# Retention and gated feed-forward on one core: another order of reading and writing in the output evacuation, one score moved by a tile, some preparation steps in another order

## The chip, the cores and the metric

The kernel runs on one core of a Trainium2 chip. The metric is the time of one execution on the device in microseconds (us), as the median of several runs. Besides, one execution was recorded by the hardware profiler; all durations of single instructions come from that one. PE is the matrix engine (PEld its weight loads), DVE the vector engine, ACT the scalar engine, POOL the general engine, SP the engine that here issues most of the DMAs.

## The reference, cut to what matters

```python
# q, k, v: [8, 8, 576, 64] f32      (batch, heads, positions, head size)
scores = q @ k.T / sqrt(64)
Dmat[i, j] = gamma_h ** (i - j) if i >= j else 0
x = (scores * Dmat) @ v             # -> [4608 tokens, 512]
h = x @ w_in                        # w_in  [512, 2048]
out = (h * cos(h)) @ w_out          # w_out [2048, 512], out [4608, 512] f32
```

## The kernel before, in words

**Retention.** Tokens are taken in 18 groups G of 256. A group has four chunks of 64 positions. The decay is taken into q and k beforehand (`prep_q`, `prep_k`, line 179, on POOL), so that a chunk needs the masked scores of its own keys (`scores`, line 286, masks at 298 or 302 on DVE), a running state k^T v (`states`, matmuls 359, additions on DVE at 380 and 382, bf16 copies `sb` on ACT at 390 and 391), and output matmuls (`retention`, line 469): "cross" and "same" of queries with the state, "own" of masked scores with values. Between "cross" and the rest stands a nop on ACT (481) that PE waits for. `done` (line 494) evacuates the outputs from PSUM as bf16 into xT, two copies of 128x512 per group: both on ACT, or one on ACT and one on DVE where it is called with `both`. From G=6 (`FINE`) on, queries lie in an order in which four neighbouring tokens are 16 places apart (r, i), and xT takes them in token order (i, r), so the copy has to permute.

k and q are turned by DMA transposes (`turn_k`, `turn_q`, line 205) into kT and qT. `values` (816) casts v to bf16 on ACT. `turned(G)` turns k of G; `quad(Q)` scales the queries of four blocks on POOL; `load`, `load_q` fetch k and v of a group, q of two groups.

**Feed-forward.** Tokens go through in ten tiles n, of 512, 256, 256 and then seven of 512 tokens (n = 3 is `S7`, n = 9 `last`). A tile n >= 3 has two parts. First `mm1` (545): 8 blocks i, each with a PSUM bank of "abm" in turn, cosine on ACT (553), product on DVE (554) into gT. Then `mm2_seven`: the second matmul as seven products of half size (697) in the order 3, 4, 5, 2, 1, 7, 6. Five of them take sums of quarters of gT (`g_sum`, line 624, gs5, gs2, gs1, gs7, gs6), on DVE where the condition `on_dve` holds, otherwise on POOL, with a fence so that a POOL sum comes after the DVE sum before it. The results are put together by ACT copies (742, 747, 752) and DVE additions (722) and stored by SP (729).

**Order of the work.** All of it is written out by hand; each engine runs its instructions in the order of the program. Into tile n >= 3 retention is woven for the next tile's tokens: groups G = 2n and G + 1, and scores for the group after. The table `at` says ahead of which product each step stands. `unit(G)` is retention(G) with the scores and states of G + 1. `begin`/`end` is retention alone; `end(both)` evacuates first on ACT, then on DVE. In tiles 3 and 4 the steps stand at products 5, 1 and 6; in tiles 5 to 7 at 4 and 1. Tile 4 has `unit` also at 6, so that it computes three scores: of 8, 9 and 10.

Preparation is called from three places: `prep_inside(n, i)` after block i of mm1, `sums_after(n, i)` after that for the g_sums, and `feed(s)` after each of the four stores r = 0 (c12), 1 (c21), 2 (u11), 3 (u22) of a tile. In `feed` n counts from 0 for tile 3, so that G = 8 + 2n is the first group of the tile after. Buffers: one gT, one gs of each kind, three of kT, of the bf16 values and of the loaded k and v each, four of scaled k.

Of the kernel before, what the change touches and what calls it, by code (L numbers as in the profile page):

```python
# [17 lines left out]
def kernel(  # L18
# [26 lines left out]
    NP = NG // 2  # L45
# [14 lines left out]
    S7 = 3  # L60
# [349 lines left out]
    def retention(G, bank="m", evac=nc.scalar.copy):  # L410

        if len(bank) == 1:
            ps = psum.tile([P, 2, 2, DG, HP], F32, tag=bank, name="ov")
            outs = [ps[:, x] for x in range(2)]
        else:
            outs = [psum.tile([P, 2, DG, HP], F32, tag=b, name="ov") for b in bank]
        vb = tiles["v", G]
        own, cross, same = [], [], []  # L420
        every = slice(0, 2)
        for y in range(2):
            ret = tiles.pop(("ret", G, y))
            yq = every if G < FINE else slice(y, y + 1)
            for h0 in range(0, H, 2):
                for x in range(2):
                    for h in (h0, h0 + 1):
                        own.append(
                            (
                                h, x, yq, HP, vb[half(x), h, y, :],  # L430
                                ret[half(x), h // HG, blocks_of(G, y, h % HG), :],
                            )
                        )
        before = (steps(G - 1) + steps(G))[-len(steps(G)) - 1 : -1] if G else [None] + steps(0)[:-1]
        for prev, (name, cells, fresh, _) in zip(before, steps(G)):
            _, x, y = name
            mix = (G, x) == (2, 0)
            if prev is None or (fresh and not mix):
                continue
            sb = tiles.pop(("sb", prev[0]))  # L440
            n = QP if mix else HP
            yq = every if y is None else slice(y, y + 1)
            for he in range(2):
                for hg in range(HG):
                    (same if he == x else cross).append(
                        (
                            he * HG + hg, x, yq, n, sb[half(he), hg, :],
                            queries(G, he, hg, x, yq, n),
                        )
                    )  # L450

        def spread(part):

            part.sort(key=lambda u: (u[2].start, u[0] % HG // 2 * 2))
            return part

        parts = {"cross": spread(cross), "own": own, "same": spread(same)}
        begun, left, turn = set(), {}, []
        for part in parts.values():
            for h, x, *_ in part:  # L460
                left[x, h % 2] = left.get((x, h % 2), 0) + 1

        def run(name, switch=False):
            i = None
            for h, x, yq, n, lhsT, rhs in parts.pop(name):
                at = (x, h % 2)
                left[at] -= 1
                dst = outs[x][half(h % 2), yq, h // 2, :n]
                i = nc.tensor.matmul(  # L469
                    dst if name == "own" else as_queries(G, dst),  # L470
                    lhsT=lhsT,
                    rhs=rhs,
                    start=at not in begun,
                    stop=left[at] == 0,
                    skip_group_check=True,
                )
                begun.add(at)
                if turn:
                    fence(i, turn.pop(), "other rows")
            if switch and i is not None:  # L480
                turn.append(nc.scalar.nop())
                fence(turn[0], i, "other rows")

        def done(*evacs):
            xT = x_of(2 * G * P, 2 * P)
            if G < FINE:
                xT = xT.rearrange("p c (x i y) -> p x y c i", x=2, y=2)
            else:
                xT = xT.rearrange("p c (y x i r) -> p x y c r i", x=2, y=2, r=4)
            for x in range(2):  # L490
                ps = outs[x]
                if G >= FINE:
                    ps = ps.rearrange("p y c (r i) -> p y c r i", r=4)
                (evacs or (evac, evac))[x](xT[:, x], ps)  # L494

        return run, done
# [109 lines left out]
    def g_sum(n, x, e0, e1):  # L606

        gT = tiles["g", n]
        a, b, op_ = {
            5: ((0, 0), (0, 1), ALU.add),  # L610
            2: ((1, 0), (1, 1), ALU.add),
            1: ((0, 0), (1, 1), ALU.add),
            7: ((0, 1), (1, 1), ALU.subtract),
            6: ((1, 0), (0, 0), ALU.subtract),
        }[x]
        if ("gs", n, x) not in tiles:
            tiles["gs", n, x] = sump.tile([P, E2, 256], BF16, tag=f"gs{x}", name=f"gs{x}")
        i0, i1 = (
            gT[:, k * E2 + e0 : k * E2 + e1, r * 256 : (r + 1) * 256] for r, k in (a, b)
        )  # L620
        on_dve = x == 5 or (n, x) == (S7, 2) or (n, x, e0) in (
            (S7, 1, 4), (S7 + 1, 2, 4), (last, 1, 0), (last, 2, 4)
        ) or (x == 6 and e0 == 0 and S7 < n < last)
        i = (nc.vector if on_dve else nc.gpsimd).tensor_tensor(  # L624
            out=tiles["gs", n, x][:, e0:e1], in0=i0, in1=i1, op=op_
        )
        if on_dve:
            tiles["gate"] = i
        elif "gate" in tiles:
            fence(i, tiles.pop("gate"), "port free")  # L630

    def sums_after(n, i):

        if n == S7:
            if i < 4:
                w_sums(3 + i % 2, i // 2 * 4, i // 2 * 4 + 4)
            elif i < 6:
                g_sum(n, 5, i % 4 * 4, i % 4 * 4 + 4)
                if i == 5:
                    g_sum(n, 6, 0, 4)  # L640
            elif i == 7:
                g_sum(n, 2, 0, E2)
                g_sum(n, 1, 4, E2)
                g_sum(n, 1, 0, 4)
                for e in (0, 4):
                    g_sum(n, 7, e, e + 4)
                g_sum(n, 6, 4, E2)
        elif n == S7 + 1 and i in (3, 7):
            for x in (5, 2):
                g_sum(n, x, i - 3, i + 1)  # L650
            if i == 7:
                g_sum(n, 6, 0, 4)
            g_sum(n, 1, i - 3, i + 1)
            if i == 7:
                for e in (0, 4):
                    g_sum(n, 7, e, e + 4)
                g_sum(n, 6, 4, E2)
        elif i == 3:
            for x in (5, 2, 1, 7) if n < last else (5, 1, 2, 7, 6):
                g_sum(n, x, 0, 4)  # L660
        elif i == 7 and n == last:
            late_sums(n)
# [155 lines left out]
    def feed(s):  # L818

        n, r = divmod(s - starts[S7] // P, 4)  # L820
        G = 8 + 2 * n
        if n == 0:
            if r == 0:
                load_q(5)
                load(10)
            elif r == 2:
                quad(4)
                turned_q(4)
                prep_k(8, 0)
                prep_k(8, 1)  # L830
                turned(8)
                values(8)
            elif r == 3:
                prep_k(9, 0)
                prep_k(9, 1)
                turned(9)
                values(9)
            return
        if G >= NP:
            return  # L840
        if r == 0:
            values(G)
            if G + 3 < NP:
                load(G + 3)
        if r < 2:
            prep_k(G + 1, r)
        if r == 1 and G + 2 < NP:
            quad(G // 2 + 1)
        if r == 2:
            turned(G + 1)  # L850
        if r == 3:
            values(G + 1)
            if G + 2 < NP:
                turned_q(G // 2 + 1)

    def prep_inside(n, i):
        G = 2 * n + 2
        if n == S7 + 1 and i == 3:
            quad(5)
        if n > S7 and i in (3, 7) and G < NP:  # L860
            prep_k(G, i // 4)
            if i == 7:
                if n == S7 + 1:
                    turned_q(5)
                turned(G)
                if n == S7 + 1:
                    load(11)
                if G + 2 < NP:
                    load_q(G // 2 + 1)
                    load(G + 2)  # L870

    plan = {
# [179 lines left out]
    for n, w in enumerate(widths):  # L1052
# [64 lines left out]
            ]  # L1117
        else:
            at = {}
            if n in (3, 4):  # L1120
                at = {
                    5: lambda acts, flush, later: (flush(), at_once(*ready(G))),
                    1: lambda acts, flush, later: unit(G, acts, flush),
                    6: lambda acts, flush, later: (flush(), begin(G + 1), end(both)),
                }
                if n == 4:
                    at[6] = lambda acts, flush, later: unit(
                        G + 1, acts, flush, lambda masks, add, copy: (masks[0](), add(), copy())
                    )
# [62 lines left out]
```

## Time and profile before

| | us |
|---|---|
| median of 5 runs | 295.71 |
| the 5 runs | 295.21, 295.32, 295.71, 296.86, 297.33 |
| the profiled execution | 295.17 |
| its span on the core | 293.5 |
| PE busy | 277.5 |
| tile 3, first to next tile's first h matmul | 86.03 to 117.70 |
| tile 4 | 117.70 to 147.74 |
| tile 5 | 147.74 to 177.22 |
| tiles 6, 7, 8 | to 206.02, to 234.65, to 263.57 |

A line of a wait list has an engine and line, what it waited for, then total us, times and the longest. A line of the chain has the start, the duration and what ran. A line of a group has the engine, the operation, out<-in, the shapes, the count, then busy us, mean ns of one and the idle time before. A line of one source line has min/median/max ns of one.

### The profile page before, as it was taken

What the parts mean: (1) busy time and instruction counts of PE and PEld (TensorE: products, weight loads), DVE (VectorE), ACT (ScalarE), POOL (GpSimd) and SP (SyncE); (2) the same over time, 40 slices, a digit from 0 to 9 for tenths busy, and PEclk for the clock granted to TensorE, in tenths of its full rate; (3) what the DMA queues carried; (4) which work ended last, traced back from release to release, by engine and by line L of the source; (5) the groups of instructions that cost most, each with busy time, mean ns of one, the idle gap of its engine ahead of it and who ended that gap; (6) DMA issues with size and microseconds to landing.
All of it is one profiled execution on the core that took longest, in us unless ns stands there. A gap on an engine that the chain in (4) does not pass through costs nothing.

```text
span 293.5 us, 8817 instructions
## 1 busy us (share of the span) xinstructions
PE 277.5 (95%) x3822; PEld 190.9 (65%) x3845; DVE 205.6 (70%) x265; ACT 164.5 (56%) x199; POOL 185.3 (63%) x161
## 2 busy tenths in 40 slices
PE   6779999899999999999999999999999999999994
PEld 2458645747658887448854875488448845784594
DVE  6766745494857987589867974798489757935872
ACT  5546414634426639463886784678467756645620
POOL 7890037671193269986956997499859906850582
PEclk9999999999999999999999999999999999999998
DMA  7999999999999999998999699919991230031013
GB/s 213 269 155 206 224 227 252 195 291 241 203 222 205 206 208 229 183 217 179 204 217 263 133 210 221 254 38 259 243 183 39 76 107 0 4 102 43 0 46 100
DMA packets 119030, 50.38 MB, mean 172 GB/s; under 512 B 83024, under 2 KB 117968, under 8 KB 118992
## 3 DMA queue, kind: packets, MB, share of 16 engines
q1 hardware_dynamic: 114224, 45.10, 73.4%
q0 software_dynamic: 4224, 4.19, 9.1%
q8 instruction: 30, 0.49, 0.7%
q10 hardware_dynamic: 544, 0.52, 0.5%
q14 instruction: 8, 0.07, 0.1%
HBM read 36.70 MB, written 9.44 MB: 157 GB/s over the span
## 4 chain that ended last, share of the span: by engine, by line
PE 74%; DMA 11%; POOL 4%; DVE 4%; ACT 2%; issue 2%; SPq 1%; DVEq 0%; POOLq 0%; ACTq 0%
PE h L545 36%; PE o L697 25%; DMA w_out_sb<-in_moe_w_out_dram 7%; PE o L562 6%; PE ov L469 3%; DMA fk<-in_k_dram 3%; DMA kT<-ks 2%; PE sc L286 2%; PE st L359 2%; POOL gs L624 1%; POOL ks L179 1%; DVE xT L494 1%; DVE ot L722 1%; POOL w_out_sb L967 1%; POOL w_in_sb L962 1%
## 5 line engine op out<-in xcount | busy, mean ns | idle before, releaser
L624 POOL TENSOR_TENSOR gs<-gT 128x1024 bf16<-128x1024 bf16 x45 | 94.5, 2129 | 56.9 <-DVE gs L624 56.9
L545 PE MATMUL h<-xT,w_in_sb 128*128 128x256 bf16 (+1 forms) x756 | 126.7, 325 | 3.7 <-DVE xT L494 3.1
L554 DVE TENSOR_TENSOR gT<-h,cosh 128x1024 bf16<-128x1024 f32 x72 | 88.0, 1223 | 47.4 <-ACT cosh L553 47.4
L553 ACT ACTIVATE cosh<-h,half_pi 128x1024 f32<-128x1024 f32 x72 | 80.2, 1114 | 58.4 <-PE h L545 58.4
L545 PEld LDWEIGHTS <-w_in_sb 128*128 128x128 bf16 x768 | 74.4, 98 | 53.2 <-issue 2.9
L697 PEld LDWEIGHTS <-gs 128*128 128x128 bf16 x576 | 54.1, 98 | 6.6 <-POOL gs L624 0.2
L179 POOL TENSOR_TENSOR qs<-fq,gq 128x512 bf16<-128x512 f32 x31 | 31.5, 1046 | 36.0 <-DMA fq<-in_q_dram 36.0
L494 ACT CAST xT<-ov 128x512 bf16<-128x512 f32 x29 | 32.7, 1228 | 12.6 <-PE ov L469 12.6
L179 POOL TENSOR_TENSOR ks<-fk,gk 128x512 bf16<-128x512 f32 x34 | 37.2, 1108 | 3.4 <-DMA fk<-in_k_dram 3.3
L697 PE MATMUL o<-ws,gs 128*128 128x256 bf16 (+1 forms) x352 | 38.4, 268 | 0.0
L562 PE MATMUL o<-w_out_sb,gT 128*128 128x512 bf16 x117 | 28.1, 379 | 1.6 <-issue 0.8
L697 PE MATMUL o<-w_out_sb,gT 128*128 128x256 bf16 x224 | 26.3, 273 | 0.0
L697 PE MATMUL o<-w_out_sb,gs 128*128 128x256 bf16 x224 | 25.8, 273 | 0.0
L722 DVE TENSOR_TENSOR ot<-o,ot 128x512 f32<-128x512 f32 (+2 forms) x32 | 19.7, 620 | 8.4 <-PE o L697 8.1
L697 PEld LDWEIGHTS <-gT 128*128 128x128 bf16 x224 | 21.5, 98 | 4.0
L562 PEld LDWEIGHTS <-gT 128*128 128x128 bf16 x128 | 11.7, 98 | 13.4 <-issue 1.0
L624 DVE TENSOR_TENSOR gs<-gT 128x1024 bf16<-128x1024 bf16 (+1 forms) x24 | 20.0, 863 | 0.4
L390 ACT CAST sb<-s 128x768 bf16<-128x768 f32 (+2 forms) x16 | 11.1, 696 | 15.8 <-DVE s L382 13.7
L722 DVE TENSOR_TENSOR ot<-ot,o 128x512 f32<-128x512 f32 x14 | 9.6, 684 | 9.4 <-ACT ot L752 8.3
L298 DVE TENSOR_TENSOR ret<-sc,tri 128x1024 bf16<-128x1024 f32 x12 | 14.5, 1212 | 0.0
L302 DVE TENSOR_TENSOR ret<-sc,tri 128x1024 bf16<-128x1024 f32 x10 | 11.9, 1217 | 2.9 <-PE sc L286 2.8
L469 PE MATMUL ov<-qT,sb 64*64 64x64 bf16 (+1 forms) x424 | 11.4, 201 | 1.1 <-ACT sb L390 0.5
(86 smaller groups left out, 190.6 us busy)
## 6 DMA issues: line engine op xcount, KB each, us to landing
out_dram<-ot SPq DMA_DIRECT2D x35, 256.0 KB, 3.7
fk<-in_k_dram SPq DMA_DIRECT2D x23, 256.0 KB, 6.6
fv<-in_v_dram SPq DMA_DIRECT2D x23, 256.0 KB, 5.2
fk<-in_k_dram SPq DMA_DIRECT2D x4, 512.0 KB, 7.4
fv<-in_v_dram SPq DMA_DIRECT2D x4, 512.0 KB, 7.4
w_in_sb<-in_moe_w_in_dram POOLq DMA_DIRECT2D x4, 512.0 KB, 8.5
w_out_sb<-in_moe_w_out_dram POOLq DMA_DIRECT2D x4, 512.0 KB, 15.5
fq<-in_q_dram SPq DMA_DIRECT2D x4, 512.0 KB, 6.8
```

The costliest lines, as they stand in the source:

```text
L179: eng.tensor_tensor(out=out_.rearrange("p (b a) d -> p a b d", a=2), in0=f.rearrange("p (a b) d -> p a b d", a=2), in1=by.rearrange("p (a ...
L298: nc.vector.tensor_tensor(out=ret, in0=ps, in1=by, op=ALU.mult)
L302: nc.vector.tensor_tensor(out=ret.rearrange(shape, r=2), in0=ps.rearrange(shape, r=2), in1=by.unsqueeze(1).to_broadcast([P, H, P]), op=ALU ...
L469: i = nc.tensor.matmul(dst if name == "own" else as_queries(G, dst), lhsT=lhsT, rhs=rhs, start=at not in begun, stop=left[at] == 0, skip_g ...
L494: (evacs or (evac, evac))[x](xT[:, x], ps)
L545: nc.tensor.matmul(ps[:, j, :], lhsT=w_in_sb[:, dg, (et + j) * P : (et + j + 1) * P], rhs=xT[:, dg], start=(dg == 0), stop=(dg == DG - 1),)
L553: nc.scalar.activation(cosh, ps, ACTF.Sin, bias=half_pi, scale=1.0)
L554: nc.vector.tensor_mul(gT[:, et : et + m, c0 : c0 + w], ps, cosh)
L562: nc.tensor.matmul(ps, lhsT=gT[:, et, tsi * P : (tsi + 1) * P], rhs=w_out_sb[:, et, :], start=(et == 0), stop=(et == ET - 1),)
L624: i = (nc.vector if on_dve else nc.gpsimd).tensor_tensor(out=tiles["gs", n, x][:, e0:e1], in0=i0, in1=i1, op=op_)
L697: nc.tensor.matmul(dst[i], lhsT=lhs[:, e, j * P : (j + 1) * P], rhs=rhs[:, e, c0:c1], start=(x in (3, 4, 1, 7) and e == 0 and (i == 0 or l ...
L722: pend.append(lambda: nc.vector.tensor_tensor(out=out_, in0=in0, in1=in1, op=op_))
```

## The change

Four things change. In `done`, for G >= 6, the copy goes through (i, r) in place of (r, i): it reads every sixteenth f32 of PSUM and writes rows of 64 bf16. In the table `at`, tile 5 gets the form that tile 4 had, and tile 4 that of tile 3: the scores and states of G = 10 move from product 6 of tile 4 to product 5 of tile 5, and retention of G = 10 and 11 from products 4 and 1 to 1 and 6. The g_sums of tile 5 follow the list of tile 4, with one sum (2, second half) on DVE. In `feed` and `prep_inside` some steps move: `values(8)`, the second `prep_k(G + 1)`, `turned(G + 1)`, `load(G + 3)`, and `load_q` ahead of `load(11)`.

```diff
@@ done
-                xT = xT.rearrange("p c (y x i r) -> p x y c r i", x=2, y=2, r=4)
+                xT = xT.rearrange("p c (y x i r) -> p x y c i r", x=2, y=2, r=4)
...
-                    ps = ps.rearrange("p y c (r i) -> p y c r i", r=4)
+                    ps = ps.rearrange("p y c (r i) -> p y c i r", r=4)
@@ g_sum
-            (S7, 1, 4), (S7 + 1, 2, 4), (last, 1, 0), (last, 2, 4)
+            (S7, 1, 4), (S7 + 1, 2, 4), (S7 + 2, 2, 4), (last, 1, 0), (last, 2, 4)
@@ sums_after
-        elif n == S7 + 1 and i in (3, 7):
+        elif n in (S7 + 1, S7 + 2) and i in (3, 7):
@@ feed
                 turned(8)
-                values(8)
             elif r == 3:
...
                 turned(9)
+                values(8)
                 values(9)
...
         if r == 0:
             values(G)
+            for y in range(2):
+                prep_k(G + 1, y)
+        if r == 1:
+            turned(G + 1)
+            if G + 2 < NP:
+                quad(G // 2 + 1)
             if G + 3 < NP:
                 load(G + 3)
-        if r < 2:
-            prep_k(G + 1, r)
-        if r == 1 and G + 2 < NP:
-            quad(G // 2 + 1)
-        if r == 2:
-            turned(G + 1)
@@ prep_inside
                 turned(G)
+                if G + 2 < NP:
+                    load_q(G // 2 + 1)
                 if n == S7 + 1:
                     load(11)
                 if G + 2 < NP:
-                    load_q(G // 2 + 1)
                     load(G + 2)
@@ the table at
-            if n in (3, 4):
+            if n in (3, 4, 5):
...
-                if n == 4:
+                if n == 5:
                     at[6] = lambda acts, flush, later: unit(
```

## Prediction

> **What bounds the kernel now.** I read the page from its first part downwards. PE is busy 95% of the span and its clock row stands at 9 in every slice but the last, so the question is only where PE stands still or does work that can go.
>
> ```profile
> PE 277.5 (95%) x3822; PEld 190.9 (65%) x3845; DVE 205.6 (70%) x265; ACT 164.5 (56%) x199; POOL 185.3 (63%) x161
> ```
>
> The diff acts from tile 3 on (101 us and later, after that tile's first matmuls). So the second view is the list of waits of PE alone, from 101 us to the end; columns are total us, times, longest us.
>
> ```profile
> PE h L545 <- DVE xT L494: 0.9, 1, 0.9
> PE sc L286 <- DMA kT<-ks: 0.7, 1, 0.7
> PE ov L469 <- ACT sb L390: 0.3, 1, 0.3
> PE st L359 <- issue: 0.3, 1, 0.3
> ```
>
> Four waits, 2.2 us together: this part of the program has little left to give. The chain of work in order of time (start us, us, what) places the first two.
>
> ```profile
> 114.37 0.62 PE ov L469 x48
> 115.01 1.31 ACT xT L494
> 116.35 1.31 DVE xT L494
> 117.66 0.04 issue
> 117.70 0.38 PE h L545
> ...
> 164.41 1.46 POOL ks L179
> 165.89 5.00 DMA kT<-ks
> 170.89 0.04 issue
> 170.94 0.45 PE sc L286 x32
> ```
>
> At the end of tile 3 the outputs of G=7 are evacuated by ScalarE and then VectorE, one after the other, and tile 4's first matmul waits for both. In tile 5 the scores of G=12 wait for a DMA transpose that POOL released late. The 0.3 us on sb is at 255 us, in tile 8, whose order the diff leaves as it is.
>
> **The evacuation.** It is two copies of 128x512 f32 for each G. The line's own view gives min/median/max ns; beside it stand the rows that I judge the new form by.
>
> ```profile
> L494 ACT CAST xT<-ov x29: 729/1308/1427, 15.2 to 259.3; 128x512 bf16<-128x512 f32 x29
> L494 DVE CAST xT<-ov x7: 717/724/1300, 15.9 to 116.3; 128x512 bf16<-128x512 f32 x7
> ```
> ```profile
> L572 ACT COPY ot<-o 128x512 f32<-128x512 f32 x8 | 4.7, 586 | 9.7 <-PE o L562 9.7
> L697 PE MATMUL o<-ws,gs 128*128 128x128 bf16 x32 | 2.1, 219 | 0.0
> ```
> ```profile
> L984 PE MATMUL tr<-ident,qs x16: 282/314/314, 6.9 to 8.8; 128*128 128x128 bf16 x16
> ```
>
> By the times in the trace the short copies (0.73 us) are those of G<6, which write every second bf16; the long ones (1.30) are those of G>=6, which write every fourth. Both read PSUM in rows. The new form writes rows and reads one f32 in sixteen. No row shows such a read. From below it can't beat the copy in rows both ways, 0.586 on ACT. The nearest row on PSUM is L984, which writes every second f32: 314 against 219 ns for the same 128 columns in rows (L697), so 0.74 ns more for each lone element, and from 0.42 (273 less 219 ns, over 128 more columns) the pace goes to 1.16 ns. ACT takes 0.91 ns an element anyhow (sb copies: 633 ns for 512, 874 for 768, so 241/256 = 0.94; 405 for 256, so 0.89) and DVE 1.04 (1217 for 1024, 686 for 512). At 1.16 ACT gains (1.16-0.91) x 512 = 0.13 on 0.59 to 0.73, DVE 0.06 on 0.69 to 0.72. So the pair costs 1.3 to 1.65 us; I take 0.70 + 0.72 = 1.42, against 2.60 now. From above, nothing in the trace holds it: a lone read may cost what the lone write costs now (1.30) or, if that extra of 0.72 is paid twice, 0.59 + 2 x 0.72 = 2.03 each. Both ends stay in the range.
>
> [...]
>
> What the pair is worth: product 6 of tile 3 starts at 114.87, and at the other tile ends h follows 1.90 after that start (145.84 to 147.74), so h could start at 116.77 and starts at 117.70: gap 0.93. With pair sum s the gap is s - 1.67, never under 0. At 1.42 it is gone, with 0.25 to spare; next is PE itself. The other evacuations lie beside products and hide as they do now.
>
> **Values(8) behind values(9).** The two 0.6 us casts (113.39 to 114.55) sit on ACT ahead of G=7's evacuation. The ACT nop that separates G=7's cross and own matmuls is queued behind them, and PE has 0.12 us idle there (3.88 busy of 4.00 from 112 to 116): -0.12. The casts are then run with values(9), at 116, where ACT was idle 2.4 us before the first cosh; v(8) is read only at 135. Cost nothing.
>
> **The third score.** Tile 4 loses scores and states of G=10, and its last unit becomes the form of tile 3; tile 5 gets tile 4's form. PE's pauses between products, from the chain: tile 3 0.75 + 1.17 + 0.95 = 2.87; tile 4 0.64 + 1.27 + 1.63 = 3.54 (the last with the 0.26 fetch wait, "issue", at 145.36); tile 5 1.21 + 2.03 = 3.24 (with the 0.68 on kT). New tile 4: 0.64 + 1.27 + (0.95 - 0.12) = 2.74, -0.80. New tile 5: 3.54 if the fetch wait stays at that place, 3.28 if not: +0.30 or +0.04. The kT wait is in this: G=12's scores come at product 6, about 3.6 us + 1.3 later than now, and kT lands where it did or sooner. The price is at the end of tile 4, which now also ends in the serial ACT and DVE pair: s - 1.67 again, nothing at 1.42, 0.93 at 2.60. Without the faster copies this edit is a loss.
>
> **g_sum of tile 5.** One sum (2, second half) goes from POOL (2.13) to DVE (0.85). POOL then runs 2, 1 before the second prep_k(12) instead of 2, 1, 7: ks(12) ends some 2.1 us sooner than 165.87. After the last gT (164.14) POOL runs 1, 7, 7, 6 from about 166.4 to 174.9, as tile 4 did with the same list from 136.09 to 144.48; product 6 starts near 176. DVE was idle enough in tile 4 with this list. Nothing.
>
> **Feed and the SP queue.** POOL's order is unchanged: prep_k(G+1) twice, then the quad. On SP turned(G+1), one DMA transpose, now stands ahead of load(G+3) (four or five DMAs) and the u11 store. In tile 4 SP is late anyway: the c12 store issues only at 150.75, and ks(11) has been ready since 146.5, so kT(11) issues near 152 instead of 157.66, and the load some 2 us later, ahead of a use a tile (28 us) later. In tiles 6 and 7 the transpose holds the stores until POOL's ks (206.4 in tile 6); their buffers come round two tiles later. load_q(6) ahead of load(11): two fq DMAs go at 135.8 instead of 141.1, and the five of load(11) 2.2 us later, so prep_k(11) may wait at 144.4 up to 2 us, but the quad behind it loses its 3.86 us wait for fq. PE reads kT(11) near 169. Nothing; price if the cover fails, one wait like today's on kT, 0.7.
>
> **Sum.** -0.93 - 0.12 - 0.80 + 0.30 = -1.55 (-1.81 without the fetch wait). The profiled execution took 295.17 (span 293.5 and 1.67 around it), 0.54 under the median of the runs shown, near the lowest, 295.21. That gives 293.6 by it and 294.2 by the median; I say 293.8. In general: -1.55 + 2 x max(0, s - 1.67) + max(0, s - 2.49), the last because tile 5 now ends, like tile 4 today, in two copies on ACT (145.25 to 147.69) just ahead of h (147.74).
>
> **Rivals.** (1) The read in steps costs what the write in steps did: s = 2.60, both gaps 0.93, sum +0.31, 295.5; s = 2.1 gives -0.7. [...] Against: L984's pace. The edit then doesn't do what it says. (2) Slower: each lone PSUM read costs twice the extra of today's write, 2.03 a copy, s = 4.06: -1.55 + 4.78 + 1.57 = +4.8, 300.0. It decides by over 0.5% (1.48 us, about what a measurement of this kernel tells from no change) from s = 2.95, 1.48 a copy. Place: the ends of tiles 3, 4 and 5. Nothing in the profile excludes it. (3) The order: fk(11), or the transpose parked at the head of SP, makes a kT late once: -1.55 + 0.7, 294.3. Against: slack of 15 us or more at kT(11).
>
> **Chances.** Fast copies 0.55, of which 0.40 beyond 0.5%, since the sum is at that bound; rival 1 (with part ways) 0.22; rival 2 0.13; rival 3 0.10. Faster 0.40, same 0.15 + 0.22 + 0.10 = 0.47, slower 0.13. Range: low 293.36 less 0.4 of scatter; high rival 1 on the median, 296.0, plus 0.4.
>
> **To look for.** ACT and DVE xT from 115 us at 0.6 to 0.8; no PE wait on xT at the ends of tiles 3 and 4; no wait on kT near 171; from first h to first h, tile 3 about 1.05 us shorter, tile 4 0.8 shorter, tile 5 up to 0.3 longer. Wrong if xT stays at 1.2 or more, if h waits for xT at two tile ends, or if a PE wait on ks, sb or gs appears in tile 5.

## The result and the profile after

The changed kernel takes 298.05 us as the median of 37 runs, the kernel before 295.64 of 72; the ratio is 1.0053, 95% interval 1.0034 to 1.0072. The forecast was 293.8 within 292.9 to 296.4: wrong, and on the other side. Ratios leave out the slow runs, those over 1.5% above the fastest of the same kernel. The first profile of the changed kernel is of a run of 300.51 us; the lines below are from a second one (run a_again, 296.09 us with a span of 294.3), and the text says so where the first had more of the same.

The evacuation does what was forecast. Its line in the changed kernel (min/median/max ns):

```profile
L494 ACT CAST xT<-ov x28: 585/592/744, 15.2 to 259.8; 128x512 bf16<-128x512 f32 x28
L494 DVE CAST xT<-ov x8: 691/726/731, 15.9 to 144.9; 128x512 bf16<-128x512 f32 x8
```

Reading every sixteenth f32 of PSUM took 0.592 us on ACT, the copy in rows (L572) takes 0.586; the 1.3 us are gone, the pair takes 1.32. In the chain at the end of tile 3, h now follows product 6 directly:

```profile
114.27 0.58 PE ov L469 x48
114.84 1.85 PE o L697 x16
116.69 0.22 PE h L545
```

PE's list of waits from 101 us on has lost the waits on xT and kT, and two others stand there:

```profile
PE ov L469 <- issue: 1.5, 1, 1.5
PE h L545 <- DVE gT L554: 1.0, 1, 1.0
PE ov L469 <- ACT sb L390: 0.3, 1, 0.3
```

The table of stages (from a tile's first h to the next tile's; columns: length, busy of PE, PEld, DVE, ACT, POOL, granted clock, DMA share, GB/s) gives tiles 3, 4 and 5:

```profile
85.94:116.53 30.59, 30.47 (x536) 26.27 (x536) 24.41 (x32) 16.45 (x23) 17.47 (x15) 1.00 1.09 212
116.53:145.92 29.39, 29.17 (x416) 19.56 (x416) 22.66 (x28) 16.16 (x22) 24.26 (x19) 1.00 1.07 199
145.92:178.26 32.34, 29.73 (x480) 20.02 (x480) 23.68 (x32) 16.73 (x24) 24.78 (x19) 1.00 1.22 229
```

Against 31.67, 30.04 and 29.48 before: tile 3 gained 1.08 (forecast 1.05), tile 4 0.65 (forecast 0.80), and tile 5 lost 2.86 (forecast 0.04 to 0.30). Everything was given back in one tile, 2.5 us of it by two waits. **The first** begins on ACT. Its order in time at the start of tile 5:

```profile
147.63 0.62 ACT L816 CAST vb<-fv 128x512 bf16<-128x512 f32 x1 [2.77 <-DMA fv<-in_v_dram]
149.25 0.62 ACT L816 CAST vb<-fv 128x512 bf16<-128x512 f32 x1 [1.00 <-DMA fv<-in_v_dram]
149.77 2.11 ACT L553 ACTIVATE cosh<-h,half_pi 128x1024 f32<-128x1024 f32 x2
```

These casts are values(11). They stand ahead of tile 5's first cosine in ACT's queue and wait for fv(11), which load(11) now issues behind load_q(6). The first cosine runs at 149.77, 3.85 us after h begins at 145.92, so PE has filled its three banks (24 matmuls of h, 23 of them in the trace) and stands 1.0 us (2.3 in the first profile, with 4.9 on ACT). In the kernel before, h began at 147.74, the casts found their data, and the first cosine came 2.35 us after h:

```profile
149.05 1.13 ACT L816 CAST vb<-fv 128x512 bf16<-128x512 f32 x2
150.09 1.11 ACT L553 ACTIVATE cosh<-h,half_pi 128x1024 f32<-128x1024 f32 x1
```

**The second** is the wait named issue: PE stands though no operand, buffer or semaphore in the profile holds it. The experiments are about these two.

### The profile page after: what moved, and what is told of

It is laid out like the page before. It is cut to its first block, busy times and chain, and to the rows that moved or that the text cites. A ratio compares the mean times of both kernels' runs of the same rounds, so it can differ in the third digit from the quotient of the medians.

```text
span 298.7 us, 8813 instructions
## 1 busy us (share of the span) xinstructions
PE 281.0 (94%) x3822; PEld 193.5 (65%) x3845; DVE 206.3 (69%) x267; ACT 148.9 (50%) x198; POOL 182.9 (61%) x160
## 4 chain that ended last, share of the span: by engine, by line
PE 83%; DVE 6%; ACT 4%; issue 3%; DMA 2%; SPq 1%; POOL 1%; DVEq 0%; ACTq 0%; POOLq 0%
PE h L545 40%; PE o L697 26%; PE o L562 8%; PE ov L469 4%; DMA fv<-in_v_dram 2%; PE st L359 2%; PE sc L286 2%; PE tr L985 1%; DVE xT L494 1%; DVE ret L302 1%; SPq L170 1%; DVE s L382 1%; DVE ot L722 1%; ACT sb L390 1%; ACT kT L241 1%
## 5 line engine op out<-in xcount | busy, mean ns | idle before, releaser
L545 PE MATMUL h<-xT,w_in_sb 128*128 128x256 bf16 (+1 forms) x756 | 128.5, 328 | 5.5 <-DVE xT L494 2.6
L624 POOL TENSOR_TENSOR gs<-gT 128x1024 bf16<-128x1024 bf16 x44 | 92.4, 2130 | 65.1 <-DVE gs L624 65.1
L494 ACT CAST xT<-ov 128x512 bf16<-128x512 f32 x28 | 16.3, 621 | 17.1 <-PE ov L469 17.1
L816 ACT CAST vb<-fv 128x512 bf16<-128x512 f32 x20 | 11.4, 617 | 5.0 <-DMA fv<-in_v_dram 5.0
```

The costliest lines, as they stand in the source:

```text
L545: nc.tensor.matmul(ps[:, j, :], lhsT=w_in_sb[:, dg, (et + j) * P : (et + j + 1) * P], rhs=xT[:, dg], start=(dg == 0), stop=(dg == DG - 1),)
L624: i = (nc.vector if on_dve else nc.gpsimd).tensor_tensor(out=tiles["gs", n, x][:, e0:e1], in0=i0, in1=i1, op=op_)
```

## Experiments

Ratios are to the kernel before, run on the same chip. Theory V is the late values, theory F the program fetch: PE would wait for the next block of its own program. A profile shows the waits of one execution; the verdicts rest on the ratios.

**a_again.** The changed kernel.

> The changed kernel unaltered, to see whether its profile repeats what the first profile of it showed. Theory V (late values): load_q(6) stands ahead of load(11) on SP, so fv(11) lands near 150 us in place of 145 or so; ACT meets values(11) at the head of its queue near 145 and waits 4 to 5 us, the cosines of tile 5 are late, PE runs out of free banks and stands 2.3 us at 151.7, and its granted clock falls afterwards. By V the wait ACT vb <- DMA fv is 3 to 5 us in this profile too and PE waits 1 to 2.5 us on gT. Theory F (fetch): what counts is the PE wait named issue, 2.0 and 0.4 us in tile 5, where PE runs into a new block of its program while the DMA engines are full; by F this wait shows at the same PE instruction in each profile and the wait on fv comes and goes. Ratio to before 1.003 to 1.010 by both.

1.0041 (1.0012 to 1.0071). Both waits came again: fv 3.8 us on ACT, 1.0 on PE, issue 1.5. But the issue wait was not at the instruction of the first profile (states of product 1's unit, 2.0): it was in the unit at product 6, where the first profile had 0.4.

**b_load_back.** Theory V undone by the order of the loads.

```diff
+                if n == S7 + 1:
+                    load(11)
                 if G + 2 < NP:
                     load_q(G // 2 + 1)
-                if n == S7 + 1:
-                    load(11)
```

> The changed kernel with load(11) ahead of load_q(6) again, as before the change. Theory V: fv(11) lands near 146, ACT waits under 1 us on it, no PE wait on gT in tile 5, ratio to before 0.993 to 0.997 (the sum of the prediction, -1.55 to -1.81 us). Theory F: the fv wait was a symptom, the issue waits of about 2 us stay, ratio 0.999 to 1.006.

1.0019 (0.9975 to 1.0064). PE's wait on gT is gone, though ACT still waits 2.5 us on fv(11), where V had under 1; and the issue wait has grown:

```profile
172.33 0.44 PE L469 MATMUL ov<-ret,vb 64*64 64x64 bf16 x30
175.64 0.22 PE L469 MATMUL ov<-ret,vb 64*64 64x64 bf16 x2 [2.88 <-issue]
```

**c_values_later.** The order of loads kept, values(11) taken out of the way of the cosines.

```diff
+        if n == S7 + 2 and i == 4:
+            values(11)
...
         if r == 3:
-            values(G + 1)
+            if n != 1:
+                values(G + 1)
```

> The changed kernel with its order of loads, but with values(11) on ACT only after the fifth block of tile 5, so that no cosine stands behind the wait for fv(11). Theory V: fv(11) lands near 150 as in the changed kernel, and yet no PE wait on gT; ratio 0.993 to 0.997. If instead the load order hurts in another way (late ks(11), DMA engines full), PE still loses 1 us or more somewhere in tile 5: ratio over 0.999. Theory F: issue waits stay, ratio 0.999 to 1.006.

1.0054 (1.0021 to 1.0088): no wait on gT, but issue waits of 1.3 (tile 4) and 0.8 (tile 5). So V's wait goes when its cause goes, but taking it away alone gives nothing that these intervals separate.

**m_shift48.** What is the issue wait? In PE's order of instructions (each matmul and each weight load counts one) it stood so far at rows 3763, 4018, 4529 and 4783, which lie 255, 511 and 254 apart: borders of 256 instructions. The page's queue "q8 instruction" moves 30 packets of 16 KB. Here 48 PE instructions are added at the start, on the order of b_load_back.

```diff
+    for _ in range(24):
+        nc.tensor.matmul(idle[:, :64], lhsT=zeros[:, :P], rhs=zeros[:, :64], start=True, stop=True)
```

> The changed kernel with load(11) ahead of load_q(6) and 24 more small warming matmuls at the start (48 PE instructions, some 2.5 us in a stretch where PE waits for q anyhow). Theory F: every border between blocks of 256 instructions comes 48 instructions sooner in the program: a wait in tile 5 stands inside the output matmuls of the unit at product 1 or early among those of the unit at product 6, not two matmuls into the states or before the last two own matmuls, where all versions with this program so far had it. By any theory that ties the wait to an operation or a buffer it stays at the states or the last own matmuls.

One execution, so a place and no ratio:

```profile
173.88 0.25 PE L469 MATMUL ov<-ret,vb 64*64 64x64 bf16 x6
177.52 0.41 PE L469 MATMUL ov<-ret,vb 64*64 64x64 bf16 x26 [3.40 <-issue]
```

In b_load_back two own matmuls were left behind the wait, here 26: 24 matmuls, 48 instructions sooner. The wait is tied to the place in the program, as F says. The packets, from the trace's DMA records: here one ran from 174.79 to 176.07 and PE went on at 177.52; in b_load_back 172.98 to 174.27 and 175.64; in a_again 173.38 to 174.69 and 175.99; in c_values_later 168.85 to 170.06 and 171.56. PE goes on 1.3 to 1.5 us after its packet is through in these four, and packets take 0.9 to 1.9 in tiles 4 and 5 of all the runs. What varies most is when the packet starts: 1.45 to 4.6 us after PE's entry into the block before, in x, v and k below.

**e_only_evac, e_again.** The evacuation's two lines alone, on the kernel before.

```diff
-                xT = xT.rearrange("p c (y x i r) -> p x y c r i", x=2, y=2, r=4)
+                xT = xT.rearrange("p c (y x i r) -> p x y c i r", x=2, y=2, r=4)
...
-                    ps = ps.rearrange("p y c (r i) -> p y c r i", r=4)
+                    ps = ps.rearrange("p y c (r i) -> p y c i r", r=4)
```

> The kernel before with the new evacuation alone. By the prediction the copies take 0.59 to 0.72 us and the PE wait of 0.9 us at the end of tile 3 goes, nothing else changes: ratio 0.996 to 0.998. Were reading PSUM in steps the cause of the loss (PE writes hindered by the strided reads), the ratio would be above 1 here.

> The kernel before with the new evacuation alone, once more, beside the three others: ratio 0.993 to 0.998, no PE wait on xT at the end of tile 3, the issue wait at the end of tile 4 anywhere from 0 to 2.6 us.

0.9957 (0.9932 to 0.9982) and 0.9962 (0.9934 to 0.9989): some 1.2 us faster, the copies at 592 and 728 ns. An issue wait of 2.6 us at row 4018 (0.26 in the profile of before) is in the first profile, a late kT (3.7) and an issue wait of 0.8 in tile 3 in the second: such waits come and go from execution to execution of one program, without the third score, too.

**f_evac_old.** The changed kernel with the old evacuation: the two lines of e_only_evac, turned back.

> The changed kernel with the old evacuation (1.3 us a copy). By the formula of the prediction the two gaps of 0.93 us at the ends of tiles 3 and 4 come back: 1.9 us above the changed kernel, ratio 1.008 to 1.014. If the gap at the end of a tile only gives the DMA engines time that PE then doesn't wait elsewhere, the ratio stays at that of the changed kernel, 1.003 to 1.007.

1.0133 (1.0056 to 1.0210, six runs), with the gaps that the prediction's formula has: 0.90 at the end of tile 3, 0.88 at tile 4's. At tile 5's end, where two copies on ACT run ahead of h, it had 0.11 and 0.43 was measured.

**k_evac_score.** Evacuation and third score on the kernel before, feed and loads untouched: e_only_evac and

```diff
-            (S7, 1, 4), (S7 + 1, 2, 4), (last, 1, 0), (last, 2, 4)
+            (S7, 1, 4), (S7 + 1, 2, 4), (S7 + 2, 2, 4), (last, 1, 0), (last, 2, 4)
...
-        elif n == S7 + 1 and i in (3, 7):
+        elif n in (S7 + 1, S7 + 2) and i in (3, 7):
...
-            if n in (3, 4):
+            if n in (3, 4, 5):
...
-                if n == 4:
+                if n == 5:
```

> The kernel before with the new evacuation and the third score moved (with its sums of tile 5), feed and loads as before. Theory F (PE's next 16 KB block of program comes over the DMA engines, about 1.0 us for its packet and 1.3 to 1.6 us more until PE goes on, and queues behind loads; where PE runs through a block in under 5 us, as in tile 5 with three units, the queueing shows as the wait named issue): issue waits of 1 to 3 us at the second or third unit of tile 5, ratio 0.998 to 1.005, clearly above the 0.996 of the evacuation alone. If the sum of the prediction holds and only the moved load hurt: no issue wait over 0.5 us, ratio 0.993 to 0.996.

1.0115 (1.0091 to 1.0138, five runs), an issue wait of 2.5 at row 4783. The stages from 174 us on (columns as above) show a second price:

```profile
174.00:176.00 2.00, 0.25 (x30) 0.25 (x31) 0.68 (x1) 0.00 (x0) 2.00 (x3) 1.00 0.97 173
176.00:178.00 2.00, 2.00 (x53) 1.62 (x40) 1.41 (x4) 1.15 (x3) 2.00 (x3) 0.79 1.07 254
178.00:180.00 2.00, 1.78 (x7) 1.03 (x7) 0.98 (x2) 2.00 (x4) 1.63 (x2) 0.50 1.03 232
```

From 177.17 on PE's granted clock is halved for 3.41 us while PE is busy, which by half of that length costs another 1.7 (an estimate).

**q_evac_feed.** Evacuation and feed without the third score's move, load(11) first: on the changed kernel, the four edits of k_evac_score turned back and the edit of b_load_back made.

> The changed kernel without the move of the third score (tables of tiles 4 and 5 and their sums as before) and with load(11) ahead of load_q(6): new evacuation and new feed order. Theory F: the program of tiles 4 and 5 is cut as in the kernel before, one issue wait in tile 4 at most, ratio 0.994 to 0.997, as with the evacuation alone. If the new order of the feed is what fills the DMA engines at the wrong time, issue waits of 1 us or more in tile 5 and a ratio over 0.999.

0.9991 (0.9959 to 1.0023). The one profile has issue waits of 0.6 in tile 4 and of 0.5 and 3.5 in tile 5, so the third score is not needed for a long wait there. The interval does not part this version from the evacuation alone, so that the feed's new order brings the wait is not shown.

**l_load14_late.** On b_load_back, tile 5's loads held until after the transpose of G=13.

```diff
                 if G + 2 < NP and n != S7 + 2:
                     load_q(G // 2 + 1)
                     load(G + 2)
...
         if r == 1:
             turned(G + 1)
+            if n == 2:
+                load_q(7)
+                load(14)
```

> The changed kernel with load(11) ahead of load_q(6), and with load_q(7) and load(14) issued after the second store of tile 5 (behind the transpose of G=13) and not after its eighth block, so that no load is under way while PE runs through the units of tile 5. Theory F: the program packets in tile 5 start within about 1.5 us of PE's entering the block before, issue waits there under 0.5 us, ratio 0.993 to 0.997. If PE's waits come from its own program (too many instructions in a short time) and not from the loads: 1 to 3 us of issue as in the version with loads, ratio 1.000 to 1.005.

1.0033 (1.0006 to 1.0061). No issue wait in tile 5, as F says; in its place POOL waits 9.0 us for fq, and in tile 6 PE waits 1.8 for a late addition on DVE and, 1.0 us of matmuls later, 0.6 for a late sum on POOL.

**s_light_before, s_light_after.** Both kernels without four loads of v.

```diff
             gate = gates.pop(0) if gates else None
+            if name == "v" and 11 <= G <= 14:
+                tiles["fv", G] = tiles["fv", 10]
+                continue
```

> The kernel before without the loads of v for G = 11 to 14 (these groups take the v of G = 10; a part of the computation is changed by that), so that in tiles 4 and 5 the DMA engines have a quarter less to load. It is the control of the next one. Theory F: the issue wait in tile 4 stays under 0.5 us; the PE waits on xT (0.9) and kT (0.7 or less) stay; ratio to before 0.994 to 1.000.

> The changed kernel without the loads of v for G = 11 to 14 (as the control, the same part of the computation changed). Theory F with V: what the change loses is all the DMA engines' backlog in tiles 4 and 5, so here nothing waits on fv(11), issue waits stay under 0.5 us, and the sum of the prediction comes out: 1.5 to 1.8 us less than the control, ratio to before 0.989 to 0.995. If PE loses through the change in another way (strided reads of PSUM, three units in tile 5), the time is that of the control or above.

A miss: 1.0074 (1.0031 to 1.0118) and 1.0090 (1.0041 to 1.0138), with issue waits of 1.6 and 1.5 in the control and 3.7 in the other. Fewer bytes don't help. Without these loads the others stand elsewhere on SP and still pile up (one store takes SP 5.95 us to issue in the control, two take 4.80 in the other); that this makes the waits is not shown.

**u_evac_shift96.** On e_only_evac, 96 PE instructions at the start, so that no block of 256 falls wholly into two units.

```diff
+    for i in range(48):
+        a, b = half(i % 2), half(i % 2)
+        nc.tensor.matmul(idle[b, :HP], lhsT=zeros[a, :HP], rhs=zeros[a, :HP], start=True, stop=True)
```

> The kernel before with the new evacuation and 48 tiny matmuls (96 PE instructions) more at the start, in a stretch where PE waits for q. Without them the blocks of 256 instructions that hold tile 4's second and third unit are run in 2.3 and 3.5 us by the rows of the trace, under the 3.6 us that a program packet needs at the least (0.9 from the border to its start, 1.05, and 1.6 until PE goes on); with them every block of tiles 3 to 5 takes 4.4 us or more. Theory F: the issue wait at the end of tile 4 (0.26 us in the first profile, 2.6 in that of the evacuation alone) goes or moves into a block with more room, ratio 0.990 to 0.995 against 0.996 for the evacuation alone. If the place of the borders does not matter: 0.995 to 0.998.

A miss: 1.0064 (1.0027 to 1.0100); issue 0.6 in tile 4 and 1.5 in tile 6, kT 1.1. More time in each block does not by itself take the waits away.

**v_hold14, x_evac_score_hold, y_evac_early14.** So the burst itself was moved: in v (on b_load_back) and x (on k_evac_score) held for one and a half products; in y (on e_only_evac) the two added loads put ahead of turned(12) instead.

```diff
                 if G + 2 < NP and n != S7 + 2:
                     load_q(G // 2 + 1)
                     load(G + 2)
...
         if r == 0:
+            if n == 2:
+                load_q(7)
+                load(14)
             values(G)
```

> The changed kernel with load(11) ahead of load_q(6), and with load_q(7) and load(14) held until the first store of tile 5 (one and a half products later than in the kernel, some 5 us; the earlier try held them 11 us and starved POOL in tile 6). Theory B (burst: PE's program packet is short if no burst of loads is being issued when it is asked for; the change brought tile 5's burst, issued from about 167 to 176, and the two packets that PE needs between 168 and 178 together): issue waits in tile 5 under 0.7 us, no new wait in tile 6, ratio 0.992 to 0.997. If three units in tile 5 are too dense whatever the loads do: issue waits of 1 us or more, ratio 1.000 to 1.005.

> The kernel before with the new evacuation, the third score moved, and load_q(7) and load(14) held until the first store of tile 5; against the same without the hold, 1.0115. Theory B: the issue wait of 2.5 us in tile 5 falls under 0.7 and with it the half clock after it, ratio 0.993 to 1.000. If the density alone counts, 1.008 to 1.014 as without the hold.

> The kernel before with the new evacuation, and with load_q(7) and load(14) brought forward, ahead of the transpose of G=12 that waits for POOL, so that the burst falls from about 161 us into the stretch in which SP and the DMA engines otherwise pause and PE fetches twice. Theory B: issue waits of 1 to 3 us in tile 5 where there were none, ratio 0.999 to 1.008 against 0.996 for the evacuation alone. If the burst does not matter: no issue wait in tile 5, ratio 0.993 to 0.998.

v: 0.9973 (0.9951 to 0.9996), with an issue wait of 1.4 where theory B had under 0.7: half a miss. x: 0.9959 (0.9932 to 0.9986) against 1.0115 without the hold, and from 101 us on PE waits for one thing, the old one of tile 8:

```profile
PE ov L469 <- ACT sb L390: 0.3, 1, 0.3
```

SP's issues in k_evac_score and then in x_evac_score_hold (start, duration, what) show what the hold does:

```profile
163.79 1.29 SPq L205 DMA_TRANSPOSE kT<-ks  x1
165.13 1.95 SPq L128 DMA_DIRECT2D fq<-in_q_dram  x2
167.13 1.73 SPq L170 DMA_DIRECT2D fk<-in_k_dram  x2
168.96 5.97 SPq L170 DMA_DIRECT2D fv<-in_v_dram  x2
```
```profile
163.69 1.45 SPq L205 DMA_TRANSPOSE kT<-ks  x1
167.06 0.37 SPq L729 DMA_DIRECT2D out_dram<-ot  x1
167.48 1.17 SPq L128 DMA_DIRECT2D fq<-in_q_dram  x2
168.69 3.04 SPq L170 DMA_DIRECT2D fk<-in_k_dram  x2
171.78 5.65 SPq L170 DMA_DIRECT2D fv<-in_v_dram  x2
```

The two DMAs of fv took SP 5.97 and 5.65 us to issue in these runs, those of fk 1.73 and 3.04. In k_evac_score PE entered the block ahead of row 4783 at about 168.4 (the unit's last states) and its packet started only at 173.01; in x PE entered at 167.8, the packet started at 169.23 and was through at 170.87, before the fv burst, and PE passed the row at 172.4 without a stop. The v run sets a limit to this reading: SP's loads began 0.3 us before PE entered the block, as in x, and yet the packet started 3.7 us after the entry (169.02 to 172.73), against 1.45 in x. So the place of the loads is not all that decides. y did not tell what it was meant to: its burst held up the transpose of G=12 instead, PE waited 8.8 us for kT, 1.0335 (1.0293 to 1.0376); of the fetch it says nothing.

**w_hold_load_fwd, x_again.** With the fetch wait gone, the late values by themselves: load_q(6) ahead of load(11) in x.

```diff
+                if G + 2 < NP and n != S7 + 2:
+                    load_q(G // 2 + 1)
                 if n == S7 + 1:
                     load(11)
                 if G + 2 < NP and n != S7 + 2:
-                    load_q(G // 2 + 1)
                     load(G + 2)
```

> x_evac_score_hold (new evacuation, third score moved, loads of tile 5 held; no fetch wait) with load_q(6) ahead of load(11) in tile 4, as in the changed kernel: the late values by themselves. Theory V: ACT waits 3 to 5 us on fv(11), PE 1 to 2.3 us on gT in tile 5; ratio to before 0.999 to 1.005, so 0.3 to 1% above x_again. If the stall gives the DMA engines time that PE would else wait for elsewhere: the ratio of x_again, 0.993 to 0.998.

> x_evac_score_hold once more, as the control beside it: ratio 0.993 to 0.998, no issue wait over 0.7 us in tiles 4 and 5.

x_again 0.9934 (0.9905 to 0.9964), w 1.0004 (0.9958 to 1.0049), so V costs about 0.7%, give or take 0.5. In w's profile (PE's list first, then ACT's):

```profile
PE h L545 <- DVE gT L554: 1.8, 1, 1.8
```
```profile
ACT vb L816 <- DMA fv<-in_v_dram: 4.4, 1, 4.4
```

## Why the prediction was wrong, step by step

- **Evacuation: right.** Pair 1.32 for the 1.42 taken, no gap at either tile end, and f_evac_old brings both gaps back at 0.9. Rival 1 and rival 2, the one on the slower side, both fell: the read in steps took 592 ns on ACT, the copy in rows 586. Loss came by another mechanism than rival 2. The working around it has slips that cost nothing here: its own terms make the pair 1.47 to 1.64, above the 1.42 that it took, and for rival 1 its formula gives +0.42, not +0.31.
- **Values(8): wrong, and hidden by luck.** Tile 3 is 1.08 shorter as a whole, for 1.05. But e_only_evac, k_evac_score and x_evac_score_hold, which leave values(8) where it was, have tile 3 at 30.58, and so has q_evac_feed, which moves it. The move is worth 0.00, not 0.12 (0.03 with the old evacuation: 31.64 in f_evac_old against 31.67): from the start of G=7's cross matmuls to that of its own ones it is 0.44 us in the kernel before and in q_evac_feed. The evacuation alone gave 1.09 for 0.93, since h follows product 6 by 1.76 and not by the 1.90 taken from the other tile ends.
- **Third score: right in its matmuls, wrong in the fetch.** In x_evac_score_hold tiles 3, 4 and 5 take 30.58, 29.26 and 29.48:

```profile
85.37:115.95 30.58, 30.46 (x536) 26.29 (x536) 24.71 (x32) 17.66 (x24) 18.06 (x15) 1.00 1.11 211
115.95:145.21 29.26, 29.15 (x418) 19.43 (x416) 22.66 (x28) 15.65 (x21) 26.02 (x20) 1.00 1.07 202
145.21:174.69 29.48, 29.48 (x482) 19.97 (x480) 22.94 (x30) 16.24 (x22) 21.08 (x14) 1.00 1.07 211
```

  -1.09 - 0.78 + 0.00 = -1.87, where the prediction had -1.81 without the fetch wait. The term that failed is "New tile 5: 3.54 if the fetch wait stays at that place, 3.28 if not: +0.30 or +0.04". The 0.26 of issue in the one profile was taken for a fixed cost of that spot. It is the end of a wait for a packet of PE's program: in the profile of before (the trace's DMA records) the packet ran from 142.88 to 143.93, and PE went on at 145.62, 1.69 us after it. In the other profiles such waits measured up to 3.7 us in tiles 4 and 5, and after those of 2.5 and more the halved clock came on top.
- **Feed and the SP queue: "Nothing" was wrong.** The step followed fk(11) to prep_k(11) and kT(11) and left out fv(11), the other half of the load that it saw going 2.2 us later. SP was through with issuing it at 146.00 in a_again, against 141.09 before: 4.9 us later. And with the new end of tile 4 ACT came to the casts at 144.86, some 4 us sooner than before, so that b_load_back, too, has ACT waiting there. The reader of fv(11), values(11), stands on ACT ahead of the cosines. The lines of before had it: the casts ran at 149.05, while the fv were being issued from 137.85 on. It also priced a failed cover at 0.7, once; w measured 0.7% of the time, 2 us.
- **Rival 3** (a transfer late by the new order) was the right kind, with the wrong transfer and a third of the price.

**What stays open.** When PE asks for a packet is not in the trace. That the wait is for PE's program is shown (the row and the packet before it); that the burst of loads holds the packet back is the reading that k against x supports, and v, where the same hold left 1.4 us, is against its being the whole cause. Why a version with fewer loads has longer waits was not found. What the feed's new order costs by itself (q against e) the intervals don't settle. The losses don't add: 0.7% by V and 1.6% by the burst, yet the changed kernel, which has both, is only 0.5% above before, and in its order of the feed the hold is worth 0.5% (v against b); no run shows why.

The fastest version is x_evac_score_hold: evacuation, third score, tile 5's loads held; 0.9934 and 0.9959 in its two series. The evacuation alone has 0.9957 and 0.9962, which the intervals do not part from it.

## What to carry to other kernels

When a load is moved, list every tile it fills and every queue its readers stand in, the cast on ACT as well as the scaling on POOL. Where PE has hardly an idle microsecond, look for waits without a releaser: here they were for PE's own program (m_shift48), and moving a burst of loads changed PE's time though no operand was late (k 1.0115, x 0.9959). Try such a burst a little later, by the shortest hold that helps: measured from PE's entry into the block, 3 us later paid here (x against k), and some 9 us later starved POOL, which stood 9.0 us for fq (l against b).

## What the runs showed of the hardware that was not expected

- PE's program came in packets of 16 KB over a DMA queue ("q8 instruction" of the page), 30 for some 7,670 instructions, so one for about 256; where PE stood 0.8 us or more it went on 1.3 to 1.6 us after the packet, and it stood up to 3.7 us (s_light_after). One border cost 2.5 us and the halved clock in k_evac_score.
- After waits of 2.3 us (the first profile of the changed kernel, on gT), 2.5 (k_evac_score), 2.6 (e_only_evac), 2.9 (b_load_back) and 3.4 (m_shift48) the granted clock was halved for 3.41 us; after 1.5 (a_again), 1.8 (w_hold_load_fwd) and 2.0 (issue, the first profile of the changed kernel) it was not, but it was in l_load14_late after 1.8 and 0.6 with 1.0 us of matmuls between them. So 2.3 us of standing still is the shortest single wait from tile 3 on that it followed.
- A PSUM read of one f32 in sixteen ran at the pace of a read in rows (592 ns in a_again against 586 on ACT), and the same copy with a bf16 write to every fourth place took 1.31 us in the kernel before. The pace of a PE write to every second f32 (L984: 314 ns, against 219 in rows), which the prediction took for a bound, did not hold for this read.
